# Linear attention, RMS norm and a gelu feed-forward layer in split float32: another order of weight conversion and weight sums beside gelu

## The chip, the cores and the metric

The kernel runs on one core of a Trainium2 chip. The metric is device time in microseconds (us). Before the change three runs gave 852.69, 856.99 and 857.6 us; their median is 856.99.

## The reference

Attention without a softmax makes one 64 x 64 matrix per batch and head, the queries go through it, each head's row is normalised, and the result goes through two matrix products with a gelu between:

```python
kv = np.einsum('bhsd,bhse->bhde', k, v)
out = np.einsum('bhsd,bhde->bhse', q, kv)
rms = np.sqrt(np.mean(out * out, axis=-1, keepdims=True) + 1e-06)
x = (out / rms * g_norm).transpose(0, 2, 1, 3).reshape(4608, 512)
h = x @ w_in                                  # 512 x 2048
g = 0.5 * h * (1.0 + erf(h / sqrt(2)))
y = g @ w_out                                 # 2048 x 512
```

There are 8 batches, 8 heads, 576 positions and 64 values per head.

## The kernel before, in words

The 4608 tokens go in 9 chunks of 512 (`NCH`), and the 2048 hidden values in 16 blocks of 128 (`NF`). To keep float32 precision, every operand of a large product is split into a high part (rounded to the type that TensorE multiplies) and a low part (the rest), and three products are summed: high x high, low x high, high x low.

One *slot* is one block of one chunk. Slots 0 to 15 are chunk 0, slots 16 to 31 chunk 1. In slot s TensorE (PE) runs `layer1(s)` (L475, 12 matmuls, into a tile `ps_h`, of which there are two) and then `layer2(s-1)` (L497, 12 matmuls: four times gh with the weight's high part, gh with its low part, gl with the high part), besides small products for the next chunk's attention: `sum_kv` (L125), `project` (L182), `fold` (L212). Between the layers stands `gelu` for slot s: ScalarE (ACT) writes gh (L487) and, at full precision, the same again into ps_h (L488); VectorE (DVE) subtracts, gl = ps_h - gh (L489). So `layer2(s)` needs gh and then gl while slot s+1 runs, after `layer1(s+1)`.

In chunks 0 and 1 (`PLAIN` = 2) the first layer is computed like this. From chunk 2 on it goes in pairs of blocks by a scheme with 7 products instead of 8 (L391); its operands are sums of weight blocks, which are prepared once, during chunk 1, and kept in DRAM (`products`).

**Chunk 0 also converts the weights.** A weight arrives as 64-bit words; four steps make its two parts: `top_w` (ACT, L438, into a tile z), `bits_w` (DVE, two instructions, L448 and L451, into a tile w), `high_w` (ACT, L459) and `low_w` (DVE, L463). The list `weights` holds 32 of them in the order of their use: in 0, in 1, out 0, in 2, out 1, in 3 and so on; number 2i-1 is the block of w_in that slot i uses and number 2i+2 the block of w_out that belongs to slot i. `convert(i)` (L731) takes 2 weights in most slots (3 in slots 4, 6, 10 and 1 in slots 12 and 13), after gelu and after `spread_work`, which is the next chunk's attention (split_q, squares, rsqrt, scale, split_x):

```python
for k, n in enumerate(now):
    bits_w(n)
    high_w(n)
    if n + 2 < len(weights):
        top_w(n + 2)
    if k:
        low_w(now[k - 1])
if now:
    low_w(now[-1])
```

**Chunk 1 also prepares the sums.** `combine(j, second)` (L329), called from `later` (L708) behind `second_layer`, handles half of one pair j of w_in blocks: the first half adds high and low parts of both blocks (L336, two instructions into tiles z), forms two sums (L353, into a tile w) and lets SyncE (SP) write three unsplit operands to DRAM; the second half forms two more sums. ACT then rounds the sums into a staging tile (L355), `x2` for first halves and `x3` for second halves, and `combined()` (L357), called at the next half, subtracts on DVE (L362) and writes the staging tile to DRAM by two DMAs (L325). Slots 17 to 27 do one half each, slots 17, 19, 21, 23 and 27 two. So each staging tile is filled again two halves later, and its DMAs must have landed by then. Tiles z and w are also those through which `store` (L502) writes a finished chunk to `out`.

Every engine runs its instructions in the order in which the code calls them; the order is written out by hand. The functions that the change touches:

Of the kernel before, what the change touches and what calls it, by code (L numbers as in the profile page):

```python
# [8 lines left out]
F32 = mybir.dt.float32  # L9
F32R = mybir.dt.float32r  # L10
# [6 lines left out]
P = 128  # L17
# [19 lines left out]
def linear_attn_rms_gelu_ffn(  # L37
# [286 lines left out]
        to = products[n // 2][:, n % 2 * DM:(n % 2 + 1) * DM]  # L324
        nc.sync.dma_start(out=to.rearrange("p (a n) -> p a n", a=2), in_=src.bitcast(F32))  # L325

    whole, stage = {}, {}

    def combine(j, second):  # L329

        if not second:
            whole.clear()
            for a in range(2):
                w = parts["in", 2 * j + a].bitcast(F32)
                whole[a] = work.tile([P, DM], I32, name="z", bufs=2).bitcast(F32)
                nc.vector.tensor_tensor(out=whole[a], in0=w[:, HI], in1=w[:, LO], op=ALU.add)  # L336
                t = parts["in", 2 * j + a].rearrange("p (a n) -> p a n", a=2)
                if a == 0:
                    product_out(j, 0, t[:, :, :HALF])
                    product_out(j, 4, t[:, :, HALF:])  # L340
                else:
                    product_out(j, 3, t[:, :, HALF:])
        a11, a12 = whole[0][:, :HALF], whole[0][:, HALF:]
        a21, a22 = whole[1][:, :HALF], whole[1][:, HALF:]
        s = work.tile([P, DM], I32, name="w", bufs=2).bitcast(F32)
        s = s.rearrange("p (a n) -> p a n", a=2)
        if second:
            adds = ((s[:, 0], a11, ALU.subtract, a21), (s[:, 1], a12, ALU.subtract, whole[2]))
        else:
            whole[2] = s[:, 1]  # L350
            adds = ((s[:, 0], a21, ALU.add, a22), (s[:, 1], s[:, 0], ALU.subtract, a11))
        for o, x, op, y in adds:
            nc.vector.tensor_tensor(out=o, in0=x, in1=y, op=op)  # L353
        t = const.tile([P, 2, 2, HALF], F32R, name=f"x{2 + second}")
        nc.scalar.copy(out=t[:, :, 0], in_=s)  # L355
        combined()
        stage[j, second] = s, t  # L357

    def combined():

        for (j, second), (s, t) in stage.items():
            nc.vector.tensor_tensor(  # L362
                out=t[:, :, 1], in0=s, in1=t[:, :, 0].bitcast(F32), op=ALU.subtract
            )
            for a, k in enumerate((6, 5) if second else (1, 2)):
                product_out(j, k, t[:, a])
        stage.clear()

    ring = {}

# [73 lines left out]
    def bits_w(n):  # L444

        low = raw.pop(n).rearrange("p (n two) -> p n two", two=2)[:, :, 0]
        z, w = zs.pop(n), ws[n]
        nc.vector.tensor_scalar(  # L448
            out=w, in0=z, scalar1=3, scalar2=None, op0=ALU.logical_shift_left
        )  # L450
        nc.vector.scalar_tensor_tensor(  # L451
            out=w, in0=low, scalar=29, in1=w, op0=ALU.logical_shift_right, op1=ALU.bitwise_or
        )
# [27 lines left out]
    def gelu(h, i=None):  # L481
        if i is None:
            gh = work.tile([P, CH], F32R, name="gh", bufs=2)
            gl = work.tile([P, CH], F32R, name="gl", bufs=2)
        else:
            gh, gl = (reused(i, F32R)[:, a * CH:(a + 1) * CH] for a in range(2))
        nc.scalar.activation(out=gh, in_=h, func=AF.Gelu)  # L487
        nc.scalar.activation(out=h, in_=h, func=AF.Gelu)  # L488
        nc.vector.tensor_tensor(out=gl, in0=h, in1=gh.bitcast(F32), op=ALU.subtract)  # L489
        return gh, gl  # L490

# [213 lines left out]

    halves = [(j, second) for j in range(NF // 2) for second in range(2)]

    def later(c, i):  # L708

        for _ in range({1: 2, 3: 2, 5: 2, 7: 2, 11: 2}.get(i, 1) if 1 <= i <= 11 else 0):  # L710
            combine(*halves.pop(0))
        if not halves:
            combined()
        if i == 9:
            sums[c] = attn[c + 1].fold()
        if i in (5, 7):
            load_kv(c + 2, (i - 5) // 2)
        if i == 9:
            attn[c + 2].load(0)
        if i == 13:  # L720
            for p in (2, 3):
                load_kv(c + 2, p)
        if i == 15:
            attn[c + 2].load(1)
        if i == 13:
            for t in range(RING):
                load_products(t)

    order = list(range(3, len(weights)))

    def convert(i):  # L731


        count = 3 if i in (4, 6, 10) else 1 if i > 11 else 2
        now = [order.pop(0) for _ in range(min(count, len(order)))]
        for k, n in enumerate(now):
            bits_w(n)
            high_w(n)
            if n + 2 < len(weights):
                top_w(n + 2)  # L740
            if k:
                low_w(now[k - 1])
        if now:
            low_w(now[-1])

    def second_layer(s):
        c, i = divmod(s, NF)
# [4 lines left out]
    for s in range(PLAIN * NF):  # L752
        c, i = divmod(s, NF)
        h[s] = layer1(attn[c], i)
        if i == 1 and c:
            store(acc.pop(c - 1), (c - 1) * CH)
        if 1 <= i <= NP and not c:
            split_kv(c + 1, (i - 1,))
        if c and i in (1, 4):
            split_kv(c + 1, (0, 1) if i == 1 else (2, 3))  # L760
        if c and i in (13, 15):
            split_kv(c + 2, (i - 13, i - 12))
        if c == 0:
            g[s] = gelu(h.pop(s))
            if i == 0:
                high_w(2)
                top_w(4)
                low_w(2)
                nc.scalar.copy(out=kv_h[0], in_=kv_f)
                nc.gpsimd.tensor_tensor(  # L770
                    out=kv_l[0], in0=kv_f, in1=kv_h[0].bitcast(F32), op=ALU.subtract
                )
            spread_work(c, i)
            convert(i)
            if s:
                second_layer(s - 1)
            spread_matmuls(c, i)
            if i in (14, 15):
                load_kv(c + 2, i - 14)
            if i == 14:  # L780
                attn[c + 2].load(0)
        else:
            spread_work(c, i)
            spread_matmuls(c, i)
            g[s] = gelu(h.pop(s))
            second_layer(s - 1)
            later(c, i)

# [52 lines left out]
    for c in range(PLAIN, NCH):  # L841
        for j in range(NF // 2):
            s = c * NF + 2 * j
            pair = layer1_pair(attn[c], j, [lambda e=e: ahead(c, j, e) for e in range(2)])
            for k, t in enumerate(pair):
                g[s + k] = gelu(t, None if j % 2 else 13 + k)
            ahead_matmuls(c, j, 0)
            due = [n for n in sorted(g) if n < s]
            second_layer(due[0])
            ahead_matmuls(c, j, 1)  # L850
            for n in due[1:]:
                second_layer(n)
            ahead(c, j, 2)
            ahead_loads(c, j)
# [45 lines left out]
```

## Time and profile before

| | |
|---|---|
| median of 3 runs | 856.99 us (852.69 to 857.6) |
| profiled execution | 856.56 us |
| its span, first to last instruction | 854.8 us |
| PE busy | 838.2 us (98%) |
| DVE busy | 495.8 us (58%) |
| ACT busy | 316.8 us (37%) |
| POOL (GpSimd) busy | 72.8 us (9%) |
| mean granted TensorE clock | 0.994 of full speed |

The span is shorter than the execution's own time by 1.76 us, which lies before the first and after the last recorded instruction. Busy shares are means over the whole span; chunks 0 and 1 fill the stretch from about 23 to 228 us, the chunks with the 7 products the rest. The times in the views are us from the span's start. A bracket at a row's end is the time that the engine was idle before it, and what released it.

### The profile page before, as it was taken

Reading aid. Unit: us, or ns where it says so; the run is one execution under the profiler, and the core shown is the slowest. Engines: PE = TensorE matmul, PEld = TensorE weight load, DVE = VectorE, ACT = ScalarE, POOL = GpSimd, SP = SyncE. Lnnn points to the kernel's source line nnn. Section 1 sums busy time; section 2 is a strip of 40 time slices with the busy share of each in tenths; the row PEclk is TensorE's granted clock in tenths of the full one; section 3 lists DMA queues with packets and bytes.
Section 4 is the critical chain, followed back from the end, with each engine's and each line's share of the span. In section 5 each row is a group of like instructions: output and inputs, shape, how many; then the busy total and the mean of one; then the engine's idle time right before and its main releaser. Section 6 shows DMA issues by size and latency. Waiting matters only on the chain.

```text
span 854.8 us, 13770 instructions
## 1 busy us (share of the span) xinstructions
PE 838.2 (98%) x5388; PEld 740.0 (87%) x5388; DVE 495.8 (58%) x988; ACT 316.8 (37%) x596; POOL 72.8 (9%) x73
## 2 busy tenths in 40 slices
PE   8999999998999999999999999999999999999998
PEld 6788778876899999998999999998999999999997
DVE  4878766567555744575447634674457545754432
ACT  3676634343352315332432333233323342323221
POOL 1210021002011101100010100110011010100000
PEclk9999999998999999999999999999999999999999
DMA  9973117676467655756676656665655565556551
GB/s 364 407 288 102 59 27 257 236 238 239 160 229 251 208 194 202 251 202 228 222 251 202 220 180 234 207 216 181 226 185 191 173 217 161 177 181 227 173 173 49
DMA packets 60595, 174.95 MB, mean 205 GB/s; under 512 B 6388, under 2 KB 16116, under 8 KB 60532
## 3 DMA queue, kind: packets, MB, share of 16 engines
q1 hardware_dynamic: 60528, 174.09, 59.2%
q8 instruction: 42, 0.69, 0.3%
q14 instruction: 21, 0.17, 0.1%
q10 hardware_dynamic: 4, 0.00, 0.0%
HBM read 149.95 MB, written 24.12 MB: 204 GB/s over the span
## 4 chain that ended last, share of the span: by engine, by line
PE 78%; DVE 8%; ACT 7%; DMA 3%; issue 2%; SPq 1%; POOL 0%; ACTq 0%; DVEq 0%
PE acc L497 39%; PE ps_h L391 33%; PE ps_a L182 2%; PE ps_h L475 2%; DMA products<-x 2%; PE ps_a L125 2%; DVE w L451 2%; ACT ps_h L488 1%; ACT gh L487 1%; DVE w L448 1%; ACT z L438 1%; DVE w L353 1%; DVE gl L489 1%; DMA w_in<-qT 1%; ACT w_in L459 1%
## 5 line engine op out<-in xcount | busy, mean ns | idle before, releaser
L497 PE MATMUL acc<-w_out,gh 128*128 128x512 f32 x704 | 220.5, 395 | 2.5 <-ACT gh L487 2.5
L391 PE MATMUL ps_h<-w_in,w_in 128*128 128x256 f32 x1392 | 176.2, 283 | 0.0
L391 PEld LDWEIGHTS ps_h<-w_in,w_in 128*128 128x128 f32 x1392 | 171.1, 192 | 0.0
L497 PE MATMUL acc<-w_out,w_in 128*128 128x512 f32 x672 | 160.1, 392 | 0.0
L497 PEld LDWEIGHTS acc<-w_out,gh 128*128 128x128 f32 x704 | 130.7, 189 | 29.8 <-ACT gh L487 4.1
L497 PEld LDWEIGHTS acc<-w_out,w_in 128*128 128x128 f32 x672 | 124.0, 188 | 24.9
L497 PE MATMUL acc<-w_out,gl 128*128 128x512 f32 x352 | 138.9, 395 | 4.2 <-DVE gl L489 4.2
L391 PEld LDWEIGHTS ps_h<-x,w_in 128*128 128x128 f32 x960 | 122.5, 191 | 4.4
L391 PE MATMUL ps_h<-x,w_in 128*128 128x256 f32 x960 | 123.9, 283 | 0.0
L487 ACT ACTIVATE gh<-ps_h 128x512 fp32r<-128x512 f32 x88 | 52.4, 595 | 157.1 <-DVE ps_h L383 146.1
L487 ACT ACTIVATE w_in<-ps_h 128x512 fp32r<-128x512 f32 x56 | 33.5, 598 | 190.1 <-DVE ps_h L383 190.1
L401 DVE COPY w_in<-ps_h 128x256 f32<-128x256 f32 x56 | 23.8, 425 | 132.2 <-PE ps_h L391 132.2
L383 DVE TENSOR_TENSOR ps_h<-ps_h,w_in 128x256 f32<-128x256 f32 x168 | 72.6, 432 | 48.0 <-PE ps_h L391 43.6
L383 DVE TENSOR_TENSOR w_in<-ps_h,w_in 128x256 f32<-128x256 f32 x168 | 71.3, 424 | 49.2 <-PE ps_h L391 47.3
L475 PE MATMUL ps_h<-x,w_in 128*128 128x512 f32 x384 | 94.0, 393 | 0.6 <-POOL x L260 0.6
L489 DVE TENSOR_TENSOR gl<-ps_h,gh 128x512 fp32r<-128x512 f32 x88 | 60.4, 687 | 51.0 <-ACT ps_h L488 46.5
L475 PEld LDWEIGHTS ps_h<-x,w_in 128*128 128x128 f32 x384 | 71.9, 189 | 16.3 <-POOL x L260 1.1
L488 ACT ACTIVATE ps_h<-ps_h 128x512 f32<-128x512 f32 x144 | 85.3, 593 | 0.0
L497 PEld LDWEIGHTS acc<-w_out,gl 128*128 128x128 f32 x352 | 66.6, 189 | 20.9 <-DVE gl L489 6.8
L170 POOL TENSOR_TENSOR ql<-q,qh 128x512 fp32r<-128x512 f32 x18 | 23.7, 1315 | 299.3 <-ACT qh L169 197.0
L489 DVE TENSOR_TENSOR w_in<-ps_h,w_in 128x512 fp32r<-128x512 f32 x56 | 38.4, 685 | 17.1 <-ACT ps_h L488 17.1
L296 POOL TENSOR_TENSOR w_in<-o,w_in 128x512 fp32r<-128x512 f32 x13 | 16.8, 1312 | 179.7 <-ACT w_in L291 179.7
(124 smaller groups left out, 638.5 us busy)
## 6 DMA issues: line engine op xcount, KB each, us to landing
w_in<-products SPq DMA_DIRECT2D x196, 512.0 KB, 4.5
kv_main<-kv_main SPq DMA_DIRECT2D x26, 512.0 KB, 6.1
w_in<-w_in SPq DMA_DIRECT2D x16, 512.0 KB, 9.0
w_out<-w_out SPq DMA_DIRECT2D x16, 512.0 KB, 9.4
products<-x SPq DMA_DIRECT2D x32, 256.0 KB, 2.5
q<-qT SPq DMA_DIRECT2D x15, 512.0 KB, 5.9
products<-w_in SPq DMA_DIRECT2D x24, 256.0 KB, 3.2
out<-z SPq DMA_DIRECT2D x18, 256.0 KB, 2.1
```

The source lines that it names most:

```text
L125: nc.tensor.matmul(out=ps[r, n * D:(n + 1) * D], lhsT=t[:, 0, r], rhs=t[:, 1, r], start=(j == 0), stop=(j == NJ),)
L170: nc.gpsimd.tensor_tensor(out=ql, in0=q, in1=qh.bitcast(F32), op=ALU.subtract)
L182: nc.tensor.matmul(out=ps[:, a:e], lhsT=w, rhs=x[:, a:e], start=(m == 0), stop=(m == 2))
L383: add = lambda out, x, y: nc.vector.tensor_tensor(out=out, in0=x, in1=y, op=ALU.add)
L391: nc.tensor.matmul(out=out, lhsT=y, rhs=x[:, z, kb], start=first and kb + i == 0, stop=kb == 1 and i == 2, skip_group_check=True,)
L401: nc.vector.tensor_copy(out=p1, in_=a[:, left])
L451: nc.vector.scalar_tensor_tensor(out=w, in0=low, scalar=29, in1=w, op0=ALU.logical_shift_right, op1=ALU.bitwise_or)
L475: nc.tensor.matmul(out=h, lhsT=parts["in", i][:, w], rhs=x, start=(m == 0), stop=(m == last))
L487: nc.scalar.activation(out=gh, in_=h, func=AF.Gelu)
L488: nc.scalar.activation(out=h, in_=h, func=AF.Gelu)
L489: nc.vector.tensor_tensor(out=gl, in0=h, in1=gh.bitcast(F32), op=ALU.subtract)
L497: nc.tensor.matmul(out=ps, lhsT=x[:, ts], rhs=parts["out", i][:, w], start=(i == 0 and m == 0), stop=(i == NF - 1 and m == 2),)
```

## The change

Chunk 0. `gelu` is cut in two: the ACT part (gh and ps_h), and `rest`, the subtraction that makes gl. `convert` keeps one weight open from slot to slot (`last`): behind the two gelu instructions ACT does high_w of the weight whose bits were made in the slot before, and top_w of the one after next; DVE makes the bits of one new weight ahead of gl, then gl, then low_w of the open weight. `spread_work` comes behind that, then the other weights of the slot. The counts move too: 3 weights in slots 2, 4, 6, 8, 1 in slots 11, 12 and 14, none in 13 and 15, 2 elsewhere. The total of 29 stays.

Chunk 1. `combine` only makes the sums; `high_sums` (ACT rounds them into a staging tile) and `low_sums` (DVE subtracts, SP writes) are functions of their own. `sum_weights`, called between gelu's ACT part and `second_layer`, puts the rounding of the last sums of the slot before behind the next gelu on ACT, and one `combine` ahead of gl on DVE. Staging has four tiles: pairs with an odd j use the tiles of `w_in0` and `w_in1`, which no plain product needs any more by then; these are also two of the four tiles into which chunk 1's slot 29 loads the first products.

```diff
-        t = const.tile([P, 2, 2, HALF], F32R, name=f"x{2 + second}")
-        nc.scalar.copy(out=t[:, :, 0], in_=s)
-        combined()
-        stage[j, second] = s, t
+        stage[j, second] = s
+
+    def high_sums():
+
+        for (j, second), s in stage.items():
+            if j % 2:
+                t = reused(second, F32R).rearrange("p (k a n) -> p k a n", k=2, a=2)
+            else:
+                t = const.tile([P, 2, 2, HALF], F32R, name=f"x{2 + second}")
+            nc.scalar.copy(out=t[:, :, 0], in_=s)
+            halved[j, second] = s, t
+        stage.clear()
...
+    def rest(gh, gl, h):
+
         nc.vector.tensor_tensor(out=gl, in0=h, in1=gh.bitcast(F32), op=ALU.subtract)
...
+    def sum_weights(i, n, gelu_rest):
+
+        high_sums()
+        for k in range(n):
+            if k:
+                high_sums()
+            combine(*halves.pop(0))
+            if not k:
+                gelu_rest()
+            low_sums()
+        if not n:
+            gelu_rest()
+            low_sums()
...
-        count = 3 if i in (4, 6, 10) else 1 if i > 11 else 2
-        now = [order.pop(0) for _ in range(min(count, len(order)))]
...
+        count = 3 if i in (2, 4, 6, 8) else 2 if i < 11 else i in (11, 12, 14)
+        now = [order.pop(0) for _ in range(count)]
+        for k, n in enumerate(now or [None]):
+            if last:
+                high_w(last[0])
+                if last[0] + 2 < len(weights):
+                    top_w(last[0] + 2)
+            if n is not None:
+                bits_w(n)
+            if not k:
+                gelu_rest()
+            if last:
+                low_w(last.pop())
+            if n is not None:
+                last.append(n)
+            if not k:
+                between()
...
             g[s] = gelu(h.pop(s))
+            n = 0 if not 1 <= i <= 11 else 2 if i in (1, 3, 5, 7, 11) else 1
+            sum_weights(i, n, lambda: g.update({s: rest(*g[s])}))
             second_layer(s - 1)
             later(c, i)
```

What this moves on ACT in chunk 0, from the gelu of slot 10 to that of slot 11 (L487 and L488 are the two gelu instructions before the change, L494 and L495 with it; CAST is high_w, the rows with z are top_w). Before:

```order
L487 ACTIVATE gh_1019<-ps_h_1006 128x512
L488 ACTIVATE ps_h_1006<-ps_h_1006 128x512
L459 CAST w_in13_1026<-w_983 128x512
L438 ACTIVATE z_1028<-w_in14_206 128x512
L459 CAST w_out12_1033<-w_990 128x512
L438 ACTIVATE z_1035<-w_out13_208 128x512
L459 CAST w_in14_1041<-w_1029 128x512
L438 ACTIVATE z_1043<-w_in15_210 128x512
L487 ACTIVATE gh_1075<-ps_h_1062 128x512
```

With the change:

```order
L494 ACTIVATE gh_1029<-ps_h_1016 128x512
L495 ACTIVATE ps_h_1016<-ps_h_1016 128x512
L466 CAST w_out12_1033<-w_986 128x512
L445 ACTIVATE z_1035<-w_out13_208 128x512
L466 CAST w_in14_1042<-w_999 128x512
L445 ACTIVATE z_1044<-w_in15_210 128x512
L494 ACTIVATE gh_1077<-ps_h_1064 128x512
```

The high part of the slot's last weight no longer stands ahead of the next gelu: it comes behind it.

On DVE in the same place, from gl of slot 10 to gl of slot 11 (L448 and L451 are bits_w, L463 is low_w, L489 is gl; with the change L455, L458, L470 and L500). Before:

```order
L489 TENSOR_TENSOR gl_1020<-ps_h_1006,gh_1019 128x512
L448 TENSOR_SCALAR w_983<-z_982 128x512
L451 SCALAR_TENSOR_TENSOR w_983<-w_in13_202,w_983 128x512
L448 TENSOR_SCALAR w_990<-z_989 128x512
L451 SCALAR_TENSOR_TENSOR w_990<-w_out12_204,w_990 128x512
L463 TENSOR_TENSOR w_in13_1026<-w_983,w_in13_1026 128x512
L448 TENSOR_SCALAR w_1029<-z_1028 128x512
L451 SCALAR_TENSOR_TENSOR w_1029<-w_in14_206,w_1029 128x512
L463 TENSOR_TENSOR w_out12_1033<-w_990,w_out12_1033 128x512
L463 TENSOR_TENSOR w_in14_1041<-w_1029,w_in14_1041 128x512
L489 TENSOR_TENSOR gl_1076<-ps_h_1062,gh_1075 128x512
```

With the change:

```order
L500 TENSOR_TENSOR gl_1030<-ps_h_1016,gh_1029 128x512
L470 TENSOR_TENSOR w_out12_1033<-w_986,w_out12_1033 128x512
L455 TENSOR_SCALAR w_1036<-z_1035 128x512
L458 SCALAR_TENSOR_TENSOR w_1036<-w_out13_208,w_1036 128x512
L470 TENSOR_TENSOR w_in14_1042<-w_999,w_in14_1042 128x512
L455 TENSOR_SCALAR w_1045<-z_1044 128x512
L458 SCALAR_TENSOR_TENSOR w_1045<-w_in15_210,w_1045 128x512
L500 TENSOR_TENSOR gl_1078<-ps_h_1064,gh_1077 128x512
```

Between the last bits of a slot and the next gl there is no low_w any more; that low_w follows gl.

On DVE in slot 17 of chunk 1, from the next batch's kv split (L138) on (L336 and L353 are the sums, L362, then L369, the low part into the staging tile). Before:

```order
L138 TENSOR_TENSOR kv_l0_76<-ps_a_1297,kv_h0_74 64x2x64 x2
L489 TENSOR_TENSOR gl_1377<-ps_h_1343,gh_1376 128x512
L336 TENSOR_TENSOR z_1397<-w_in0_377 128x512
L336 TENSOR_TENSOR z_1401<-w_in1_397 128x512
L353 TENSOR_TENSOR w_1404<-z_1401 128x256
L353 TENSOR_TENSOR w_1404<-w_1404,z_1397 128x256
```

With the change:

```order
L138 TENSOR_TENSOR kv_l0_76<-ps_a_1297,kv_h0_74 64x2x64 x2
L336 TENSOR_TENSOR z_1380<-w_in0_377 128x512
L336 TENSOR_TENSOR z_1384<-w_in1_397 128x512
L353 TENSOR_TENSOR w_1387<-z_1384 128x256
L353 TENSOR_TENSOR w_1387<-w_1387,z_1380 128x256
L500 TENSOR_TENSOR gl_1377<-ps_h_1343,gh_1376 128x512
```

Four instructions of the sums now stand ahead of gl.

## Rows read from the trace of the kernel before

**Rows 1.** Windows view: busy us (instructions) of each engine, granted clock, DMA share, GB/s.

```profile
23.00:122.00 99.00, 94.77 (x481) 75.59 (x480) 79.94 (x140) 63.33 (x121) 11.74 (x9) 1.00 0.47 178
122.00:228.00 106.00, 100.87 (x573) 81.82 (x572) 65.32 (x120) 40.82 (x79) 12.72 (x10) 0.97 0.65 221
228.00:840.00 612.00, 612.00 (x4124) 557.22 (x4124) 336.32 (x695) 201.02 (x377) 43.52 (x34) 1.00 0.60 203
```

**Rows 2.** Timeline of PE: starts of layer 1, slots 12 to 16, 25, 26, 28 to 30.

```profile
96.41 2.88 PE L475 MATMUL ps_h<-x,w_in 128*128 128x512 f32 x12
...
110.16 2.88 PE L475 MATMUL ps_h<-x,w_in 128*128 128x512 f32 x12
...
115.60 2.88 PE L475 MATMUL ps_h<-x,w_in 128*128 128x512 f32 x12
...
121.66 2.88 PE L475 MATMUL ps_h<-x,w_in 128*128 128x512 f32 x12
...
177.30 2.88 PE L475 MATMUL ps_h<-x,w_in 128*128 128x512 f32 x12
...
185.14 0.41 PE L212 MATMUL ps_a<-part,fold 128*128 128x64 f32 x2 [0.61 <-DVE part L205]
185.35 3.01 PE L475 MATMUL ps_h<-x,w_in 128*128 128x512 f32 x12
...
196.36 2.88 PE L475 MATMUL ps_h<-x,w_in 128*128 128x512 f32 x12
...
203.34 2.88 PE L475 MATMUL ps_h<-x,w_in 128*128 128x512 f32 x12
...
214.88 3.28 PE L475 MATMUL ps_h<-x,w_in 128*128 128x512 f32 x12
```

**Rows 3.** Timeline of PE: waits in slots 2, 13 and 29.

```profile
41.90 0.27 PE L182 MATMUL ps_a<-qh,kv_h 128*128 128x64 f32 x1 [1.43 <-DVE kv_l L138]
...
106.56 0.73 PE L497 MATMUL acc<-w_out,gh 128*128 128x512 f32 x2 [0.83 <-ACT gh L487]
...
210.44 0.79 PE L497 MATMUL acc<-w_out,gl 128*128 128x512 f32 x1 [2.41 <-DVE gl L489]
```

**Rows 4.** Timeline of ACT and DVE around the gelu of slot 12.

```profile
103.72 0.62 ACT L459 CAST w_out<-w 128x512 fp32r<-128x512 f32 x1 [4.06 <-DVE w L451]
...
105.94 0.57 ACT L487 ACTIVATE gh<-ps_h 128x512 fp32r<-128x512 f32 x1
```

**Rows 5.** Lines view: DVE's steps of converting a w_out weight: busy us, mean ns.

```profile
L448 DVE TENSOR_SCALAR w<-z 128x512 int32<-128x512 int32 x32 | 14.7, 460 | 1.0 <-ACT z L438 0.7
...
L451 DVE SCALAR_TENSOR_TENSOR w<-w_out,w 128x512 int32<-128x512 int32 x16 | 11.1, 693 | 0.5
L463 DVE TENSOR_TENSOR w_out<-w,w_out 128x512 fp32r<-128x512 f32 x16 | 11.0, 689 | 2.8 <-ACT w_out L459 2.7
```

**Rows 6.** Timeline of ACT, DVE and POOL in slots 25, 28 and 29.

```profile
179.56 0.62 ACT L355 CAST x<-w 128x512 fp32r<-128x512 f32 x1 [4.01 <-DMA products<-x]
...
204.37 0.62 ACT L355 CAST x<-w 128x512 fp32r<-128x512 f32 x1 [4.76 <-DMA products<-x]
...
206.31 1.26 POOL L296 TENSOR_TENSOR x<-o,x 128x512 fp32r<-128x512 f32 x1 [33.52 <-PE ps_h L475]
206.37 1.75 DVE L250 TENSOR_TENSOR o<-o,sq 128x512 f32<-128x512 f32 x1
...
209.71 0.68 DVE L489 TENSOR_TENSOR gl<-ps_h,gh 128x512 fp32r<-128x512 f32 x1
```

**Rows 7.** Windows view of slot 29, columns as in Rows 1.

```profile
209.50:215.50 6.00, 5.05 (x12) 3.99 (x13) 5.58 (x10) 4.18 (x8) 1.50 (x2) 0.50 0.94 361
```

**Rows 8.** Timeline of PE and DVE in slots 17 and 18.

```profile
134.08 2.88 PE L475 MATMUL ps_h<-x,w_in 128*128 128x512 f32 x12
...
135.33 0.69 DVE L336 TENSOR_TENSOR z<-w_in 128x512 f32<-128x512 f32 x1 [0.55 <-DMA out<-z]
...
136.52 0.42 DVE L353 TENSOR_TENSOR w<-w,z 128x256 f32<-128x256 f32 x1
```

More of the change, by code (lines that the diff above doesn't have):

```diff
@@ L325, in product_out @@
         nc.sync.dma_start(out=to.rearrange("p (a n) -> p a n", a=2), in_=src.bitcast(F32))
-    whole, stage = {}, {}
+    whole, stage, halved = {}, {}, {}
     def combine(j, second):
@@ L353, in combine, with low_sums @@
             nc.vector.tensor_tensor(out=o, in0=x, in1=y, op=op)
-        t = const.tile([P, 2, 2, HALF], F32R, name=f"x{2 + second}")
-        nc.scalar.copy(out=t[:, :, 0], in_=s)
-        combined()
-        stage[j, second] = s, t
-    def combined():
-        for (j, second), (s, t) in stage.items():
+        stage[j, second] = s
[8 more added lines that the diff above has]
+        stage.clear()
+    def low_sums():
+        for (j, second), (s, t) in halved.items():
             nc.vector.tensor_tensor(
@@ L366, in combined @@
                 product_out(j, k, t[:, a])
-        stage.clear()
+        halved.clear()
     ring = {}
@@ L488, in gelu @@
         nc.scalar.activation(out=h, in_=h, func=AF.Gelu)
+        return gh, gl, h
+    def rest(gh, gl, h):
         nc.vector.tensor_tensor(out=gl, in0=h, in1=gh.bitcast(F32), op=ALU.subtract)
@@ L706, in linear_attn_rms_gelu_ffn @@
     halves = [(j, second) for j in range(NF // 2) for second in range(2)]
+    def sum_weights(i, n, gelu_rest):
[10 more added lines that the diff above has]
+            low_sums()
     def later(c, i):
[L710 to L713, printed above, removed]
         if i == 9:
@@ L729, in linear_attn_rms_gelu_ffn, with convert @@
     order = list(range(3, len(weights)))
-    def convert(i):
-        count = 3 if i in (4, 6, 10) else 1 if i > 11 else 2
-        now = [order.pop(0) for _ in range(min(count, len(order)))]
[L736 to L744, printed above, removed]
+    last = [2]
+    def convert(i, gelu_rest, between):
+        count = 3 if i in (2, 4, 6, 8) else 2 if i < 11 else i in (11, 12, 14)
[15 more added lines that the diff above has]
+                between()
     def second_layer(s):
@@ L764, in linear_attn_rms_gelu_ffn, with between @@
             g[s] = gelu(h.pop(s))
[L765 to L774, printed above, removed]
+            def between():
+                if i == 0:
+                    nc.scalar.copy(out=kv_h[0], in_=kv_f)
+                    nc.gpsimd.tensor_tensor(
+                        out=kv_l[0], in0=kv_f, in1=kv_h[0].bitcast(F32), op=ALU.subtract
+                    )
+                spread_work(c, i)
+            convert(i, lambda: g.update({s: rest(*g[s])}), between)
             if s:
@@ L845, in linear_attn_rms_gelu_ffn @@
             for k, t in enumerate(pair):
-                g[s + k] = gelu(t, None if j % 2 else 13 + k)
+                g[s + k] = rest(*gelu(t, None if j % 2 else 13 + k))
             ahead_matmuls(c, j, 0)
```

## The prediction

> **What bounds the kernel now.** I read the windows view first, by stage. From 228 us on PE is busy for all of 612.00 us at full granted clock, and the change touches nothing there; in chunk 0 it is busy for 94.77 of 99.00 us and in chunk 1 for 100.87 of 106.00, with a clock of 0.97 in the second [rows 1]. So whatever can be won lies in chunks 0 and 1. Busy time hides part of it, since matmul ends are modelled; I therefore take PE's timeline and compare the starts of layer 1 in slots that hold the same 24 matmuls. Slot 14 is a clean one: 115.60 - 110.16 = 5.44 us, 2.72 for each layer. Against it [rows 2]:
> - slots 12 and 13: 110.16 - 96.41 = 13.75, that is 2.87 more than two clean ones;
> - slot 15: 121.66 - 115.60 = 6.06, 0.62 more;
> - slot 25: 185.35 - 177.30 = 8.05, less 5.44 and less the fold's 0.21 (185.35 - 185.14): 2.40 more;
> - slot 29: 214.88 - 203.34 = 11.54, 6.10 more.
>
> Slot 2 has a wait of 1.43 us ahead of `project`, for kv_l from DVE [rows 3]. The sum is 2.87 + 0.62 + 2.40 + 6.10 + 1.43 = 13.42 us. Losses under 0.5 us in other slots are not counted.
>
> The reader should next see who is late in each. In slot 13 PE waits for gh [rows 3], which ACT makes at 105.94 although layer 1 of slot 12 ended at 96.41 + 2.88 = 99.29: 6.65 us late [rows 2, 4]. ACT was not overloaded; it sat idle for 4.06 us before a high_w, waiting for DVE's bits, with the gelu queued behind [rows 4]. The two engines run in step: gelu, gl, bits, high_w of the last weight, top_w, the next gelu. This chain is longer than a slot, and the lag grows until it is longer than PE's slack. In slots 25 and 29 it is another thing: ACT stands for 4.01 and 4.76 us before filling a staging tile whose DMAs have not landed, and the gelu stands behind it [rows 6]. In slot 29 gl then comes at 209.71, PE waits 2.41 us for it [rows 3], and the granted clock falls to 0.50, that is to 1.2 GHz, for the 6 us from 209.5 [rows 7], after PE had stood idle. So part of the 6.10 is the slow clock, and it goes with the wait.
>
> **The change part by part.** *Chunk 0, order.* The number of weights, 29, stays, so no engine's work changes; only what stands ahead of what. The gelu on ACT loses the last weight's high_w and top_w ahead of it, gl on DVE loses that weight's low_w, and DVE has one weight's bits (0.46 + 0.69 = 1.15 us) to do while ACT runs the two gelu instructions, a time in which it used to idle. One weight costs DVE 0.46 + 0.69 + 0.69 = 1.84 us [rows 5]; three and gl and one small step make about 6.9, two about 5.1, so a pair of slots needs some 12 us, and two PE slots give 10.9 and the one projection that falls in every even one, about 0.9 more. That is nearly even for slots 2 to 9 and loose later. Over the chunk DVE's 79.94 us [rows 1] must fit into 99.00 less the won 4.92: 85%. What keeps it off the path is slack: gl(s) is due only after layer 1 of slot s+1 and the two gh matmuls (two of the twelve in 2.72, 0.45), 3.2 us after layer 1 of slot s has ended, plus projections. Working the first slots through by hand with these durations, I find gl of slots 1 to 6 at least 1.7 us ahead of its use. So the 2.87 and the 0.62 go.
>
> *Slot 2.* Its kv_l step stood behind two low_w and an idle stretch for gelu; now one low_w fewer is ahead of it. By hand it ends at about 39.6, where PE before could start only at 41.90 [rows 3]; PE is ready for it at about 40.4. The 1.43 go, with 0.8 us to spare.
>
> *A weight's low part one slot later.* low_w of w_out block 1 now stands behind gl of slot 1. By hand it ends at about 36.0, and PE needs it at about 37.1. I cost it at nothing; the cover is 1 us there, 2 us in slot 3, and more from slot 4 on, when the counts have moved conversion ahead of use. If the cover is gone, PE pays the difference in two or three slots: at most 2 us.
>
> *Chunk 1, four staging tiles.* A tile is filled again after two and a half slots at the earliest, that is after 13.6 us, and the longest stand in the trace for one to land is 4.76 us [rows 6]. The 2.40 and the 6.10 go, the slow clock with them. The loads of the first products into two of these tiles now wait for staging DMAs; they have slots 30 and 31, 10.9 us, to hide in.
>
> *Chunk 1, sums ahead of gl.* This is the cost that I see. In each of slots 17 to 27 up to 2.1 us of sums (L336 twice and L353 twice) are put ahead of gl. gl is due 5.44 + 2.72 + 0.45 = 8.6 us after its slot's start, so 2.1 us hide, except where the sums wait. In slot 17 they do: the second L336 waits for a DMA of `out` and starts at 135.33, the second L353 at 136.52 [rows 8]. That takes 0.42, and gl 0.68 [rows 6], so gl ends at 137.62, or 0.1 sooner where two steps overlap. PE needs it at 134.08 + 2.72 + 0.45 = 137.25. I take a new wait of 0.35. Bounds: 0 if the DMA lands 0.4 sooner, 2 if it lands 1.6 later.
>
> *Slot 28.* Two scale steps stand ahead of gl before and after the change; from the first L250 to gl they take 209.71 - 206.37 = 3.34 us, with the transpose in front some 4. That L250 takes 1.75 us while POOL runs for 1.26 beside it; an L463, also with two inputs from SBUF, takes 0.69 [rows 5, 6]. With gelu on time and about 1.5 us of sums left from slot 27, gl ends some 6 us after the slot's start, 2.6 before it is due.
>
> The Trainium skill, in "SBUF — State Buffer", section "Who interferes with whom", has a rule that speaks against the change: a VectorE instruction with two SBUF inputs and a GpSimd instruction that reads SBUF exclude each other, and the loser stands still altogether. The 1.75 us agree with it. By that rule each of the four GpSimd splits of chunk 0 can fall on a conversion step that used to lie in an idle stretch, and would hold DVE for up to its own 1.3 us; that is the mechanism of rival two below.
>
> Sum: 856.56 (the profiled execution; 0.43 under the median) - 13.42 + 0.35 = **843.5 us**. If the small losses go as well it is about 1 us less.
>
> **The rivals.**
>
> *One: slot 29 keeps its wait.* DVE might be late in slot 28 for itself: rsqrt, four scales and three halves of sums fall in slots 26 to 28. For it: the L250 of 1.75 us and POOL's work beside it. Against it: 2.6 us of slack by hand, and an ACT that was held by a DMA, not by DVE. If it holds, 6.10 come back: 849.6.
>
> *Two: chunk 0 stays bound by the step of ACT and DVE.* Nothing is won in slots 2, 12, 13 and 15 if DVE's backlog grows past 3.2 us, because its pair of slots takes 12 us and POOL's four splits take 1.3 each from it. For it: the even balance above. Against it: DVE was 81% busy, with idle stretches that the change fills, and the counts are lower from slot 10 on. Then 4.92 come back: 848.4.
>
> *Three, slower.* gl behind sums in eleven slots. If DVE starts its sums later than 8.6 - 2.1 - 0.7 = 5.8 us after a slot's start, PE waits for gl in each; at 2 us each, which by the row of slot 29 is about where the clock falls as well, it costs 11 x 2 = 22 us against 13.4 won: 865. It needs a standing backlog in chunk 1, and DVE is busy there for only 65.32 of 106 us [rows 1].
>
> *The change doesn't do what it says* is no rival here: the rows of ACT and DVE show the gelu ahead of the last weight's high part and four staging tiles.
>
> **How the numbers follow.** My forecast 0.73, rival one 0.12, rival two 0.10, rival three 0.05. The likeliest is 843.5; it moves from 842 (small losses gone) to 846 (2 us for late weights or a late `out` DMA), and rivals one and two lie at 848.4 and 849.6. The three runs before spread by 4 us to one side of their median, so I open the low end to 840. Range 840 to 849.8. A measurement of this kernel can tell about 1% from no change, 8.6 us, so faster means below 848.4. The forecast and a part of rival two and of rival one (with less than its full 6.10) give 0.80 for that, the rest of both 0.15 for no difference, rival three 0.05 for slower.
>
> **What would show it.** Right: starts of layer 1 5.44 us apart in slots 12 to 14 and 5.65 in slot 25; slot 29 at 5.4 with a granted clock of 1.00; no ACT wait for the DMAs of `products` in chunk 1; no PE wait for kv_l; a PE wait of a few tenths for gl in slot 18; the paired products starting near 214 us instead of 228. Wrong: PE waits for gl in several slots from 17 to 27 (rival three), for gl in slot 29 only (one), for gh in slots 8 to 13 (two), or a PE wait for the low part of a w_out block in slots 2 and 3. A time below 840 would mean that chunks 2 to 8 gained too, for which I see no cause.

## The result, and the profile after

The changed kernel takes 842.9 us (median of four runs, 842.86 to 846.37), beside 856.75 us for the kernel before (four runs, 852.69 to 857.6). The ratio is 0.9853, with a 95% interval of 0.9818 to 0.9889, so it is faster by more than the 1% that can be told. The profiled execution took 842.86 us, its span is 841.1 us.

The windows view of the changed kernel, with the stretches of [rows 1] and slot 29 of [rows 7], shows where it came from:

```profile
23.00:122.00 99.00, 98.38 (x538) 80.44 (x538) 81.31 (x141) 64.80 (x124) 13.19 (x10) 1.00 0.48 181
122.00:228.00 106.00, 106.00 (x623) 89.85 (x622) 73.92 (x135) 45.27 (x89) 12.77 (x9) 1.00 0.72 246
195.45:200.89 5.44, 5.44 (x25) 4.50 (x24) 5.02 (x8) 3.87 (x8) 1.47 (x1) 1.00 0.78 218
```

PE was busy for 94.77 and 100.87 us in the first two stretches; now it is for 98.38 of 99.00 and 106.00 of 106.00, at full clock. Slot 29 is a clean 5.44 us. PE's starts, which answer to [rows 2]:

```profile
94.48 2.88 PE L482 MATMUL ps_h<-x,w_in 128*128 128x512 f32 x12
99.92 2.88 PE L482 MATMUL ps_h<-x,w_in 128*128 128x512 f32 x12
...
110.80 2.88 PE L482 MATMUL ps_h<-x,w_in 128*128 128x512 f32 x12
116.24 1.07 PE L482 MATMUL ps_h<-x,w_in 128*128 128x512 f32 x4
...
171.88 2.88 PE L482 MATMUL ps_h<-x,w_in 128*128 128x512 f32 x12
177.32 0.33 PE L212 MATMUL ps_a<-part,fold 128*128 128x64 f32 x2
177.46 3.01 PE L482 MATMUL ps_h<-x,w_in 128*128 128x512 f32 x12
...
195.45 2.88 PE L482 MATMUL ps_h<-x,w_in 128*128 128x512 f32 x12
200.89 2.88 PE L482 MATMUL ps_h<-x,w_in 128*128 128x512 f32 x12
...
213.31 0.88 PE L398 MATMUL ps_h<-x,w_in 128*128 128x256 f32 x6
```

Slots 12, 13 and 15 take 5.44 us each (slot 12: 99.92 - 94.48; slot 15: 116.24 - 110.80), slot 25 5.58 with its fold, and the paired products begin at 213.31 where they began at 227.70. That lead stays as it is through chunks 2 to 8. What PE still waits for, by the view of waits (total us, times, longest):

```profile
PE ps_a L125 <- DMA w_out<-kv_main: 1.2, 3, 0.6
PE ps_h L555 <- DVE warm L525: 1.1, 1, 1.1
PE ps_h L482 <- POOL x L260: 0.6, 1, 0.6
```

No gh, gl or kv_l stands among them any more; the waits of [rows 3] are gone.

### The profile page after: what moved, and what is told of

The parts are those of the page before. It is cut to its first block, busy times and chain, and to the rows that moved or that the text cites. A ratio compares the mean times of both kernels' runs of the same rounds, so it can differ in the third digit from the quotient of the medians.

```text
span 841.1 us, 13781 instructions
## 1 busy us (share of the span) xinstructions
PE 833.4 (99%) x5388; PEld 739.8 (88%) x5388; DVE 498.4 (59%) x988; ACT 316.1 (38%) x596; POOL 73.0 (9%) x73
## 4 chain that ended last, share of the span: by engine, by line
PE 97%; DMA 1%; DVE 1%; ACT 0%; SPq 0%; POOL 0%; issue 0%
PE acc L508 47%; PE ps_h L398 34%; PE ps_h L482 10%; PE ps_a L182 3%; PE ps_a L125 2%; DMA w_in<-qT 1%; PE acc L588 0%; SPq L99 0%; DVE w L458 0%; PE ps_a L212 0%; POOL x L260 0%; ACT gl L630 0%; DVE w L455 0%; DVE o L641 0%; DVE w L517 0%
## 5 line engine op out<-in xcount | busy, mean ns | idle before, releaser
L508 PE MATMUL acc<-w_out,gl 128*128 128x512 f32 x352 | 137.1, 390 | 0.0
L494 ACT ACTIVATE gh<-ps_h 128x512 fp32r<-128x512 f32 x88 | 52.6, 597 | 206.0 <-DVE ps_h L390 146.7
L494 ACT ACTIVATE w_in<-ps_h 128x512 fp32r<-128x512 f32 x56 | 33.5, 598 | 190.0 <-DVE ps_h L390 190.0
L500 DVE TENSOR_TENSOR gl<-ps_h,gh 128x512 fp32r<-128x512 f32 x88 | 60.4, 686 | 43.3 <-ACT ps_h L495 39.0
L495 ACT ACTIVATE ps_h<-ps_h 128x512 f32<-128x512 f32 x144 | 85.4, 593 | 0.0
L508 PEld LDWEIGHTS acc<-w_out,gl 128*128 128x128 f32 x352 | 66.1, 188 | 14.2 <-DVE gl L500 0.2
L500 DVE TENSOR_TENSOR w_in<-ps_h,w_in 128x512 fp32r<-128x512 f32 x56 | 38.4, 685 | 17.1 <-ACT ps_h L495 17.1
```

The source lines that it names most:

```text
L508: nc.tensor.matmul(out=ps, lhsT=x[:, ts], rhs=parts["out", i][:, w], start=(i == 0 and m == 0), stop=(i == NF - 1 and m == 2),)
```

## The experiments

**The measure.** The changed kernel, profiled twice, began slot 2 at 33.97 and at 35.72 us; that difference lies in slot 0 and ahead of it, and it is as large as some effects sought here. So each experiment is read by two stretches of PE's timeline, from its one profiled execution, as well: from the start of layer 1 in slot 2 to that in slot 16 (chunk 0), and from there to the first paired product (chunk 1). The kernels of the first four rows under the changed one ran beside 857.23 us for the kernel before, the next four beside 857.09, the last four beside 858.04.

| kernel | chunk 0, us | chunk 1, us | time, us | ratio to before, 95% |
|---|---|---|---|---|
| before | 87.66 | 106.04 | 856.75 | |
| changed | 82.27 | 97.07 | 842.90 | 0.9853 (0.9818 to 0.9889) |
| before with four staging tiles | 87.74 | 97.07 | 849.27 | 0.9904 (0.9883 to 0.9925) |
| changed with two staging tiles | 82.27 | 97.11 | 845.66 | 0.9868 (0.9846 to 0.9889) |
| chunk 0 changed alone | 82.27 | 104.94 | 852.76 | 0.9952 (0.9934 to 0.9969) |
| chunk 1 changed alone | 87.77 | 97.21 | 849.33 | 0.9906 (0.9883 to 0.9928) |
| changed, once more | 82.27 | 97.10 | 844.80 | 0.9866 (0.9845 to 0.9886) |
| two tiles, once more | 82.27 | 97.38 | 845.39 | 0.9866 (0.9848 to 0.9884) |
| two tiles, gl ahead of the sums | 82.27 | 102.71 | 849.06 | 0.9909 (0.9892 to 0.9925) |
| high part ahead of gelu | 84.98 | 97.08 | 846.82 | 0.9885 (0.9869 to 0.9902) |
| bits behind gl | 83.45 | 97.13 | 844.46 | 0.9840 (0.9817 to 0.9863) |
| old counts | 82.27 | 97.07 | 844.55 | 0.9844 (0.9818 to 0.9869) |
| before with the new counts | 87.84 | 107.23 | 859.21 | 1.0013 (0.9997 to 1.0030) |
| every sum twice | 82.27 | 110.36 | 857.60 | 0.9995 (0.9977 to 1.0013) |

### Four staging tiles alone

In `combine` of the kernel before:

```diff
-        t = const.tile([P, 2, 2, HALF], F32R, name=f"x{2 + second}")
+        if j % 2:
+            t = reused(second, F32R).rearrange("p (k a n) -> p k a n", k=2, a=2)
+        else:
+            t = const.tile([P, 2, 2, HALF], F32R, name=f"x{2 + second}")
```

> The kernel before with four staging tiles and nothing else. My theory (slots 25 and 29 wait only because ACT stands for the DMAs of a staging tile): the 2.40 and 6.10 us go, about 848 us, slot 29 near 5.4 us with the granted clock at 1.00; the waits of slots 2, 12, 13 and 15 stay. Rival one (DVE holds gl of slot 28 by its own queue): slot 29 keeps about half or all of its 6.1 us, 851 to 854 us.

Chunk 1 falls to 97.07 us, exactly what the whole change reaches. ACT still stands for landings, 2.15 us at the longest, where it stood 4.01 and 4.76 us in [rows 6]; PE waits for nothing in that stretch. The theory holds: in chunk 1 the tiles alone are enough.

### The new order with two tiles, and both again side by side

In `high_sums` of the changed kernel:

```diff
-            if j % 2:
-                t = reused(second, F32R).rearrange("p (k a n) -> p k a n", k=2, a=2)
-            else:
-                t = const.tile([P, 2, 2, HALF], F32R, name=f"x{2 + second}")
+            t = const.tile([P, 2, 2, HALF], F32R, name=f"x{2 + second}")
```

> The changed kernel with two staging tiles instead of four. If the tiles are what freed slots 25 and 29, their waits come back: about 851 us. If the order is enough by itself (the rounding of the last sums now stands behind the gelu on ACT, so an ACT that waits for a DMA holds no gelu up), little comes back: 843 to 845 us, with ACT waits for the DMAs of products in the trace but no PE wait of over 0.5 us in chunk 1.

The order alone reaches 97.11 us in chunk 1 as well. Its time of 845.66 was not measured beside the 842.9 (the kernel before took 857.23 beside the one and 856.75 beside the other), so the two were run again side by side:

> The changed kernel once more, as the measure for the three others of this call. Ratio to the kernel before 0.984 to 0.987, 842 to 845 us; starts of layer 1 in slots 12 to 15 5.44 us apart, paired products from 213 to 214 us.

> The changed order with two staging tiles, beside the changed kernel. Theory (either remedy alone is enough: behind the gelu ACT may stand for a landing of up to 4.8 us without holding PE): within 0.6 us of the changed kernel, no wait of PE for gh or gl in slots 17 to 31. Rival (four tiles save something on top, as 845.66 against 842.9 of two different calls suggests): 1.5 to 3 us more than the changed kernel.

844.80 (844.08 to 847.72) against 845.39 (843.95 to 847.45): no difference that can be told. The stretches differ by 0.3 us, all of it in slot 18: there the sums ahead of gl began 0.60 us after the slot's start instead of 0.32, because the DMA of `out` that they wait for landed later, and gl ended 4.18 us after it. Each remedy of chunk 1 is enough by itself, and the second adds nothing to the first. The 2.8 us between the first two figures were not the tiles.

### Each chunk's change alone

The first of these kernels has the new `convert` with the old `combine` and `later`; the second the old `convert` with the new sums and four tiles.

> The new order of gelu and conversion in chunk 0; chunk 1 as before, with two tiles. Theory (the terms of slots 2, 12, 13 and 15 are 4.92 us and add to those of chunk 1): 851.6 us, starts of layer 1 5.44 us apart in slots 12 to 14, slots 25 and 29 as long as before. Rival two (DVE too busy): 855 to 857 us.

> Chunk 0 as before; the new order of the sums and four tiles in chunk 1. Theory: the 8.5 us of slots 25 and 29 go, 848 us, and with chunk0_only's gain the two make up the whole. Rival three (sums ahead of gl cost a wait in several slots): above 850 us, with PE waits for gl in slots 17 to 27.

Chunk 0 gives 5.39 us by its stretch and 4.5 by the medians, chunk 1 8.8 and 7.9. Together 14.2 of the 14.36 that the whole change gives from slot 2 to the paired products: the parts add up, and neither needs the other. With chunk 0 alone changed, the waits of slots 25 and 29 are there, nearly as before: the slots take 7.69 and 11.17 us, where they took 8.06 and 11.53 (PE's timeline, the wait in slot 29):

```profile
206.43 0.79 PE L501 MATMUL acc<-w_out,gl 128*128 128x512 f32 x1 [2.42 <-DVE gl L493]
```

### Two tiles, with gl ahead of the sums

In `sum_weights` of the changed kernel with two tiles:

```diff
         high_sums()
+        gelu_rest()
         for k in range(n):
             if k:
                 high_sums()
             combine(*halves.pop(0))
-            if not k:
-                gelu_rest()
             low_sums()
         if not n:
-            gelu_rest()
             low_sums()
```

> Two staging tiles, the rounding of the last sums still behind the next gelu, but the sums behind gl again. Theory (what frees PE from the landings is the rounding behind gelu; sums ahead of gl are worth nothing, because gl has over 2 us to spare in slots 18 to 27): as the changed order with two tiles, 843 to 845 us, and gl of slot 17 about 2 us ahead of its use instead of 0.2. Rival (the sums ahead of gl are what makes the rounding early enough): waits of PE for gh or gl in slots 25 or 29 again, 846 to 850 us.

Chunk 1 takes 102.71 us, 5.6 more than with the sums ahead of gl: the theory falls. The rival's reason, a rounding that comes too late, holds for one rounding. The wait that the rival expected is short, 0.48 us for gl in slot 29, and slot 25 stays at 5.58 us; 4.7 of the 5.6 us lie in slot 30. ACT's timeline, of this kernel and then of the one with the sums ahead of gl, at the same instruction:

```profile
190.15 0.62 ACT L360 CAST x<-w 128x512 fp32r<-128x512 f32 x1 [2.39 <-DVE w L353]
196.57 0.62 ACT L291 CAST x<-o 128x512 fp32r<-128x512 f32 x1 [5.80 <-DMA products<-x]
```

```profile
187.89 1.13 ACT L360 CAST x<-w 128x512 fp32r<-128x512 f32 x2
193.53 0.62 ACT L291 CAST x<-o 128x512 fp32r<-128x512 f32 x1 [4.51 <-DVE o L250]
```

L291 is not part of the sums: it fills `x2` as an operand of chunk 2. With two staging tiles the last pair's sums lie in that same tile, so L291 waits for their landing, and the gelu of slot 28 stands behind L291. With the sums ahead of gl the last first half is rounded directly behind the slot's first rounding (the two at 187.89); with gl first DVE makes its sums later, and it comes at 190.15. Counted from the start of slot 2 (34.07 us in the first fence's run, 34.87 in the second's) it ends 2.55 us later. SP then issued the last write of this tile at 192.46, and L291 stood until it was in at 196.5, 4.0 us after. In the second run that write was issued at 191.08; L291 begins at 193.53 and the profile names another releaser, so the landing was in by then at the latest. So a later rounding and a slower landing both have a part. From 196.57 the lateness runs on: gelu of slot 28 at 197.62, the last low part at 199.34, SP's last `products` writes behind it, and only then, in SP's order, the loads of the next keys and values, from 201.26 where the changed kernel has them from 196.90. PE waits for those in slot 30, and the clock falls behind the waits (PE's timeline, then the windows view):

```profile
206.20 0.69 PE L125 MATMUL ps_a<-kv_main 112*64 112x64 f32 x16 [1.42 <-DMA kv_main<-kv_main]
...
208.44 0.69 PE L125 MATMUL ps_a<-kv_main 112*64 112x64 f32 x16 [1.43 <-DMA kv_main<-kv_main]
```

```profile
207.60:213.61 6.01, 5.17 (x33) 4.16 (x33) 3.25 (x7) 1.66 (x4) 0.00 (x0) 0.72 0.99 402
```

With four tiles the last pair uses the tiles of `w_in0` and `w_in1`, and in the changed kernel that L291 runs at 187.99 without a wait. So with two tiles a place for the sums matters that with four does not: the kernel before with four staging tiles has its sums behind gl too and takes 97.07 us.

### Chunk 0: the high part ahead of the gelu again

In `convert` of the changed kernel (the added lines stand at its end):

```diff
-            if last:
+            if last and (k or i == 0):
                 high_w(last[0])
                 if last[0] + 2 < len(weights):
                     top_w(last[0] + 2)
...
+        if last:
+            high_w(last[0])
+            if last[0] + 2 < len(weights):
+                top_w(last[0] + 2)
```

> The changed kernel, but in chunk 0 the rounding (high_w) and top_w of a slot's last weight stand ahead of the next gelu again; only its low part stays behind gl. Theory (the step of ACT and DVE, with the gelu behind DVE's bits, is what made slots 12, 13 and 15 late): 2 to 4.5 us of the gain in chunk 0 are lost, 845 to 847.5 us, with waits of PE for gh or gl in chunk 0 and ACT idle for DVE's w by microseconds ahead of high_w. Rival (the lower counts of weights from slot 10 on, or the low part behind gl, are enough): 842.5 to 844 us, starts in slots 12 to 15 5.44 us apart.

Chunk 0 loses 2.71 us, half of its gain. The medians measured side by side differ by 2.0, but their intervals overlap, so the stretch decides. The theory holds in size, with the place moved: the late slots are 3, 8 and 10 (0.57, 0.99 and 1.12 us over the changed kernel), while 12 to 15 are clean. In the view of waits ACT stands idle for DVE's bits (w) ahead of a high part (w_out, w_in):

```profile
ACT w_out L466 <- DVE w L458: 13.7, 12, 2.1
...
ACT w_in L466 <- DVE w L458: 7.6, 7, 1.5
```

With the change as it is these two rows read 2.8 and 2.7 us in three waits each.

### Chunk 0: the bits behind gl

In `convert` of the changed kernel:

```diff
-            if n is not None:
-                bits_w(n)
             if not k:
                 gelu_rest()
+            if n is not None:
+                bits_w(n)
```

> The changed kernel, but in chunk 0 gl stands ahead of the new weight's bits. From the start of layer 1 in slot 2 to that in slot 16 the changed kernel takes 82.27 us, the one before 87.66. Theory (the rounding behind the gelu is what unlocks ACT; DVE comes to gl late anyway, with the gelu done, so bits ahead of gl fill no idle time): 82.3 to 82.8 us, 842.5 to 845 us in all. Rival (the bits ahead of gl, done while ACT runs the gelu, are needed for DVE to keep up): DVE idles 0.8 us ahead of gl in each slot, waits of PE for gl or gh, 84 to 87 us, 845 to 849 us in all.

Chunk 0 takes 83.45 us, 1.18 more, between the two expectations; the total, 844.46, shows nothing. All of it lies in slots 2 and 3 (0.22 and 0.97 us), and PE does not wait for gl there. In slot 2 it waits for the low part of w_out block 1, which DVE now ends at 37.38 us (timeline of DVE and of PEld, PE's loading of weights):

```profile
36.69 0.69 DVE L470 TENSOR_TENSOR w_out<-w,w_out 128x512 fp32r<-128x512 f32 x1
37.43 0.19 PEld L508 LDWEIGHTS acc<-w_out,gh 128*128 128x128 f32 x1 [0.34 <-DVE w_out L470]
```

This is the cover of 1 us from the prediction's "A weight's low part one slot later", used up. In slot 3 `sum_kv` needs a tile `ps_a`, which is free once DVE's kv_l step has read it, and that step ran late (PE's and DVE's timeline in slot 3):

```profile
48.12 0.23 DVE L138 TENSOR_TENSOR kv_l<-ps_a,kv_h 64x64 fp32r<-64x64 f32 x1 [0.27 <-ACT kv_h L137]
48.45 0.69 PE L125 MATMUL ps_a<-w_out 112*64 112x64 f32 x16 [0.90 <-issue]
```

That `ps_a` is what "issue" hides is my reading of this order in time, and no run takes it apart; slot 3 with the high part ahead shows the same order (kv_l ends at 51.14, `sum_kv` begins at 51.24). From slot 4 on the place of the bits is worth nothing.

### Chunk 0: the counts, undone and alone

In `convert` of the changed kernel; in the kernel before it is the reverse:

```diff
-        count = 3 if i in (2, 4, 6, 8) else 2 if i < 11 else i in (11, 12, 14)
+        count = min(3 if i in (4, 6, 10) else 1 if i > 11 else 2, len(order))
```

> The changed kernel with the old counts of weights per slot (3 in slots 4, 6 and 10, 1 in slots 12 and 13). Theory (order and counts share the work: with the high part ahead of the gelu but the new counts the slots 12 to 15 were clean and slots 3, 8 and 10 late): waits are few, under 1 us in all, from slot 2 to slot 16 82.3 to 83.3 us, 843 to 845.5 us in all. Rival (the counts do most, since DVE has no time for a weight in slots 12 and 13): waits of PE for gl or gh in slots 11 to 13, 84 to 86 us, 845 to 848 us in all.

> The kernel before with the new counts alone (3 weights in slots 2, 4, 6, 8, one in 11, 12 and 14). Theory (the step of ACT and DVE is as long as before and needs as long a stretch; fewer weights late only move the lateness ahead): from slot 2 to slot 16 85 to 87 us against 87.66, with waits of PE in slots 3 to 10 and slots 12 to 15 5.44 us apart; 854 to 857 us in all. Rival (the counts alone take the loss away, 2.87 + 0.62): 84.0 to 84.3 us, with the wait for kv_l in slot 2 as the only one left; 852 to 853.5 us in all.

With the old counts and the new order chunk 0 takes 82.27 us, what the changed kernel takes. With the new counts and the old order it takes 87.84: slots 12, 14 and 15 are clean, slot 13 is 0.48 us late, slots 8 and 10 are 0.59 and 1.36 late, and slot 2 still waits 1.45. 1.6 of the 87.84 are a clock that fell in slot 3 (last section); without that fall it would be 86.2, inside the theory's 85 to 87. The counts move the lateness and remove little of it. The total missed its 854 to 857 by 2 us. The kernel before took 1.3 us more beside it than the 856.75 from which the theory started, and in the profiled execution (857.9) the fall and a chunk 1 longer by 1.2 us, nearly all in slot 16 where PE waits for x, were added; one profile does not tell the share of each in the median.

### Chunk 1: every sum made twice

In `combine` of the changed kernel:

```diff
-                nc.vector.tensor_tensor(out=whole[a], in0=w[:, HI], in1=w[:, LO], op=ALU.add)
+                for _ in range(2):
+                    nc.vector.tensor_tensor(out=whole[a], in0=w[:, HI], in1=w[:, LO], op=ALU.add)
...
-        for o, x, op, y in adds:
+        for o, x, op, y in 2 * adds:
```

> The changed kernel with every sum of chunk 1 made twice (some 2.1 us more of DVE in a slot, all ahead of gl for its first half). Theory (gl of slot 17 has 0.2 us to spare, because project stands between; gl of slots 18 to 27 has 2 to 6 us): PE waits about 1.9 us for gl in slot 18, perhaps up to 1 in slot 19, none after slot 20; from slot 16 to the paired products 98.5 to 101 us instead of 97.07, the upper end if the clock falls after the wait; 844.5 to 847.5 us in all. Rival (the prediction's third: a standing backlog, gl late in most of eleven slots): waits in six slots or more, 105 to 120 us, 851 us or more in all.

PE's timeline, its waits in chunk 1:

```profile
135.59 0.50 PE L509 MATMUL acc<-w_out,gl 128*128 128x512 f32 x1 [1.81 <-DVE gl L501]
162.81 0.50 PE L509 MATMUL acc<-w_out,gl 128*128 128x512 f32 x1 [0.22 <-DVE gl L501]
171.67 0.50 PE L509 MATMUL acc<-w_out,gl 128*128 128x512 f32 x1 [3.12 <-DVE gl L501]
...
195.11 0.50 PE L509 MATMUL acc<-w_out,gl 128*128 128x512 f32 x1 [0.22 <-DVE gl L501]
210.43 0.50 PE L509 MATMUL acc<-w_out,gl 128*128 128x512 f32 x1 [2.56 <-DVE gl L501]
```

Slot 18 waits 1.81 us, as the theory said. Slots 22, 23, 27 and 29 it did not see: DVE carries a backlog from slot to slot, and it is busy for 8.64 of the 8.85 us of slot 23. Chunk 1 takes 13.3 us more, 7.9 of them these waits; of the rest 3.6 lie in slots 18 and 29, where the granted clock was 0.83 and 0.84 over the slot. So the theory falls in its main point, and the rival's price (105 to 120 us for the stretch, 851 us or more in all) is right, though with five waits in place of six or more. The prediction's third rival is a real mechanism; as the change stands, DVE has the time.

## Why the prediction was right

843.5 us was predicted, 842.9 measured, 842.86 in the profiled execution that the sum speaks of. By its steps, each slot of the changed kernel against the same slot of the kernel before:

| term | predicted | measured |
|---|---|---|
| slots 12 and 13 | -2.87 | -2.87 |
| slot 15 | -0.62 | -0.62 |
| slot 25 | -2.40 | -2.47 |
| slot 29, with its slow clock | -6.10 | -6.10 |
| slot 2, kv_l | -1.43 | -1.48 |
| small losses, not counted | 0 | -0.83 (slot 8 0.40, slot 30 0.40, slot 9 0.03) |
| new wait in slot 18 | +0.35 | 0 |
| other slots, and rounding | 0 | +0.01 |
| sum | -13.07 | -14.36 |
| end of the kernel | 0 | +0.68 |

- **The wait in slot 18 is the step that failed.** The prediction put gl's due time at 134.08 + 2.72 + 0.45, as if layer 2 followed layer 1 at once. PE runs `project` between them in this slot, and the trace of the kernel before had shown it (PE's timeline, with the first use of gl):

```profile
136.79 0.22 PE L182 MATMUL ps_a<-qh,kv_h 128*128 128x128 f32 x1
...
138.12 0.39 PE L497 MATMUL acc<-w_out,gl 128*128 128x512 f32 x1
```

  PE's and DVE's timeline of the changed kernel (answers to [rows 8]):

```profile
128.68 2.88 PE L482 MATMUL ps_h<-x,w_in 128*128 128x512 f32 x12
129.00 0.69 DVE L336 TENSOR_TENSOR z<-w_in 128x512 f32<-128x512 f32 x1 [4.06 <-DMA out<-z]
130.23 0.69 DVE L336 TENSOR_TENSOR z<-w_in 128x512 f32<-128x512 f32 x1 [0.55 <-DMA out<-z]
...
131.40 0.22 PE L182 MATMUL ps_a<-qh,kv_h 128*128 128x128 f32 x1
...
131.87 0.69 DVE L500 TENSOR_TENSOR gl<-ps_h,gh 128x512 fp32r<-128x512 f32 x1
...
132.26 0.64 PE L508 MATMUL acc<-w_out,gh 128*128 128x512 f32 x2
...
132.74 0.39 PE L508 MATMUL acc<-w_out,gl 128*128 128x512 f32 x1
```

  project takes 131.40 to 132.26, 0.86 us. So gl is due 4.06 us after the slot's start, not 3.17; it ends 3.88 after it, 0.34 later than forecast. The sums do wait for the DMA of `out`, as said, and 0.18 us are left. That is little: in two other executions with the same order the sums came later, and slot 18 took 0.15 us more (chunk 1 changed alone) and 0.29 (two tiles, once more). The doubled sums show the other side of that edge: about 2.1 us more on DVE in this slot, and PE waits 1.81.
- **The small losses** of slots 8 and 30 went as well, as the text allowed ("about 1 us less"). They and the missing wait make the start of the paired products 1.3 us earlier than the sum has it.
- **The end gave half of it back.** From DVE's last copy to the span's end it is 841.1 - 836.70 = 4.40 us now, and 854.8 - 851.08 = 3.72 before: the last write to `out` landed 2.72 us after its issue, where it took 2.04 before. The order of the work there is the same, and nothing shows that the 0.7 us belong to the change: over the fourteen profiled executions of the kernels in the table that write takes from 2.03 to 4.30 us, 2.04 with the bits behind gl and 4.30 with chunk 1 changed alone. What makes it slow or fast stays open.
- **The nearness of the total is in part luck.** 1.3 us more were won than the sum has, and 0.7 came back at the end. Measured again, the changed kernel took 844.80 us. The slots of the sum, not its last digit, bear the prediction out.
- **Chunk 0.** The mechanism is as told: putting high_w back ahead of the gelu brings back 2.71 of the 5.39 us and ACT's idle stretches. The prediction wrote the gain to the order as a whole, and with the old counts the order alone does reach 82.27 us. Undone one at a time, with the rest in place, the high part behind the gelu (with top_w, which goes along) is worth 2.71, the bits ahead of gl 1.18, the counts nothing. These are not shares: neither of the first two brings back the late slots 12, 13 and 15, and which piece of the order cures those is not shown. For slot 2 the low part behind gl is the piece left over: the wait for kv_l stays away with the high part put back and with the bits put back; no run moves the low part alone. The 12 us of DVE's work for a pair of slots did fit: DVE was busy for 70.29 of the 82.27 us, 85% as forecast.
- **Slots 2 and 3.** kv_l was forecast to end at about 39.6 and ended at 39.54; the low part of w_out block 1 was forecast at 36.0 and ended at 35.98 (DVE's and POOL's timeline):

```profile
35.30 0.68 DVE L470 TENSOR_TENSOR w_out<-w,w_out 128x512 fp32r<-128x512 f32 x1
36.01 1.30 POOL L170 TENSOR_TENSOR ql<-q,qh 128x512 fp32r<-128x512 f32 x1 [4.78 <-ACT qh L169]
36.08 1.50 DVE L455 TENSOR_SCALAR w<-z 128x512 int32<-128x512 int32 x1
...
39.31 0.23 DVE L138 TENSOR_TENSOR kv_l<-ps_a,kv_h 64x64 fp32r<-64x64 f32 x1 [0.27 <-ACT kv_h L137]
```

  Here POOL's split falls on a conversion step, as rival two feared: L455 takes 1.50 us beside POOL's 1.30 where it takes 0.43 alone. Two more of the four splits, from 60.20 and 71.96 on, do the same to a low part, which takes 0.69 alone (DVE's timeline):

```profile
60.48 1.56 DVE L470 TENSOR_TENSOR w_out<-w,w_out 128x512 fp32r<-128x512 f32 x1
72.25 1.56 DVE L470 TENSOR_TENSOR w_in<-w,w_in 128x512 fp32r<-128x512 f32 x1
```

  Before the change only one split met a conversion step. The three cost DVE 2.8 us in all and PE nothing, since gl of slots 1 to 6 still came at least 1.9 us ahead of its use (1.7 forecast). L455 has one tensor input, not two. The Trainium skill, "SBUF — State Buffer", section "Who interferes with whom", says that besides instructions with two SBUF inputs a VectorE tensor_scalar can also take the ports that VectorE shares with GpSimd, in one of its faster modes; the trace agrees as far as a one-input step is held beside POOL's and ends 0.27 us after it.
- **Chunk 1, four tiles.** The 2.40 and 6.10 were written to the tiles. That is right but not the whole: the order with two tiles recovers 8.93 us (106.04 - 97.11) of the same 8.97, because ACT then stands for a landing behind the gelu and not ahead of it. The prediction asked of each part what it removes, and did not ask whether two parts remove the same wait.
- **Sums ahead of gl.** In the changed kernel gl of slots 18 to 27 ends 2 us or more ahead of its use; in slot 28 at 195.37, against 198.6 needed, 3.2 ahead where 2.6 was forecast. Rival one did not come.

## What to carry to other kernels

When an engine that runs in order stands ahead of an urgent instruction, the wait can be shortened (more buffers) or put behind the urgent one (order); test each alone, since one may be enough and their gains need not add. Count everything that the late engine's customer does in between before calling something due: 0.86 us of project decided here whether PE waited. And give a buffer's next user its own line in the account: with two tiles the landing came back through an operand of the next chunk, which merely shares the tile's name.

## What the runs showed that was not expected

The granted clock fell behind short waits in some executions and not in others. In slot 2 the kernel before waits 1.43 us for kv_l [rows 3] and runs the next slot at 1.00; with the new counts alone it waits 1.45 us at the same place and runs the next slot at 0.78, a mean over time at 1.2 and at 2.4 GHz (windows view, slot 3 of before, then of the kernel before with the new counts):

```profile
42.92:49.19 6.27, 6.27 (x45) 4.98 (x43) 4.86 (x10) 4.41 (x10) 0.14 (x1) 1.00 0.75 299
```

```profile
42.89:50.77 7.88, 7.88 (x45) 6.13 (x43) 6.37 (x13) 5.39 (x12) 0.00 (x0) 0.78 0.61 245
```

That is 1.6 us for the same work, more than the wait itself. The kernel with chunk 1 changed alone, whose chunk 0 is that of before, shows the same: a wait of 1.45 us, then 7.88 us at 0.78. The kernel before with four staging tiles waits 1.48 us there and runs the next slot at 1.00. With every sum twice, a wait of 3.12 us was followed by no fall and one of 1.81 by a slot at 0.83. So a wait's length alone did not tell whether the clock falls, and one profile does not give what a wait costs. The prediction's third rival took 2 us as about the place where the clock falls, from the one row of slot 29; these runs do not bear that out. That in slot 29 the slow clock goes with the wait is shown by every run in which that wait is gone.
